# Graph tensor product on one core: table building beside the routing loops, and a chunk's spread emitted in two half-steps

## The chip, the cores and the metric

The kernel runs on one NeuronCore of one Trainium2 chip. The metric is the device time of one execution in microseconds (us), less is better. Below, PE is the tensor engine, DVE the vector engine, ACT the scalar engine, POOL the GpSimd engine and SP the engine that issues most plain DMAs. "L547" is line 547 of the kernel before.

## The reference

There are N = 10000 nodes with 64 channels of 4 components each, and E = 640000 edges with random source and destination. Each edge carries 4 components `Y` and 4 features.

```python
R = _silu(edge_feat @ w_rad)                              # (E, C)
xs = x[src]                                               # (E, C, M)
tp = jnp.einsum('eci,ef,ifo->eco', xs, Y, cg)             # (E, C, M)
msg = R[:, :, None] * tp
agg = _segment_sum(msg.reshape(-1, C * M), dst, N).reshape(N, C, M)
return jnp.einsum('ncm,cd->ndm', agg, w_mix)
```

The costly parts are the gather by `src` and the sum by `dst`, both over random indices.

## The kernel before

The edges are first sorted by destination, in two passes, so that the sum by destination becomes dense matrix products over buckets of 32 nodes. A record of an edge is 9 words: a key that packs source and destination, `Y`, and the features.

**Three splits.** The edges are cut into three splits (0.3, 0.355 and 0.345 of them). Each split goes through pass 1, pass 2 and the messages, and later splits add to the sums of earlier ones.

**Pass 1** (`pass1`) sorts the records of a split into 18 groups of 576 nodes in DRAM (`grp`), and **pass 2** (`pass2`) sorts each group into 18 buckets (`bkt`). Together a (split, group) pair is called a segment. There are 54 segments, and the small group of 7 buckets comes first in each split.

**Tables and route.** Both passes have the same two parts. `tables` (L306 to L462) computes from digit counts where each row of output goes. It is a serial chain of small steps: a matmul on PE into the one PSUM tile with the tag `misc`, a copy by ACT or DVE, some small DVE operations of 18 to 400 columns, the next matmul. The four matmul groups that matter here are `cnt` (L320), `prep` (L341 to L343), `stp` (L404) and `ovp` (L444 to L446). As `misc` has one buffer, a stream takes it with `bank` (L135) and gives it back by setting `held` to None; the final mix of the messages uses it too. `route` (L464) then goes over chunks of 12 (pass 1) or 11 (pass 2) tiles of 128 records. Per chunk, `spread` (L516) makes a slot mask (DVE, L521), the spread records X (DVE, L524), and one-hot rows `oh` (half of them on DVE, L533, the others on ACT as six squares, L539, and one Relu, L540); a step later `move` (L543) multiplies them on PE, then `evict` copies the result out of PSUM (ACT, L554), and `store` writes it by an indirect DMA on POOL (L558). `places` (L475) holds a second one-buffer PSUM tile, with the lock `pos`, from an odd step to the next even one. X and `oh` have three buffers each, shared by the two passes.

**Messages** (`messages`, L737) run over 939 units, one per bucket and split, of 5 or 6 tiles each. Per unit POOL gathers x by source (L781), DVE builds S (L815, L818) and the products with the radial factor (L825), PE sums into PSUM (L836), DVE or ACT takes the sums out (L865, L867), and in the last split PE mixes the channels (L884). A unit is emitted in four quarters.

**Order.** In the first phase (`p1`), which runs pass 1 of the first split, only SP has a hand-written order; the other engines are ordered by a planner. The clears of `bkt` and of the later groups are woven in on SP: 0.75 clears for each step that the pass yields. In the second phase (`p2`), PE, DVE and ACT execute strictly in the order in which the generators are stepped in `groups` (L916). Before each quarter of the messages, pass 1 of the next split is advanced as far as its due time asks (counted in chunks), and pass 2 of the next segment by its share of `pass2_steps`; a step's yield says its weight, 4 (`HEAVY`) for a chunk. In pass 2, a segment's tables are built first and its route runs after them. In pass 1, the tables of the next block are advanced between the chunks, without a yield of their own when they are not yet needed. The third phase (`p3`) handles overflowing records in two short loops.

## Time and profile before

| | |
|---|---|
| time, median of 3 runs | 10816.96 us (10789.08 to 10847.26) |
| profiled execution, its own time | 10910.27 us |
| its span, first to last instruction | 10908.5 us |
| PE busy | 8286.5 us, 76% of the span |
| DVE busy | 6989.5 us, 64% |
| POOL busy | 6043.2 us, 55% |
| ACT busy | 4039.2 us, 37% |
| granted PE clock, mean | 0.84 |
| DMA traffic | 1057.34 MB, mean 97 GB/s |

Busy times are of one profiled execution; a group's row gives busy time, mean duration of one instruction, then the idle time of its engine just before it and what ended most of that idle time. No engine is busy throughout, so what matters is which waits follow each other.

### The profile page before, as it was taken

How to read it: one execution, taken by the hardware profiler on the slowest of the kernel's cores; microseconds unless marked ns; L12 is line 12 of the kernel's file. 1: busy time of each engine (PE TensorE's matmuls, PEld its weight loads, DVE VectorE, ACT ScalarE, POOL GpSimd, SP SyncE). 2: the span in 40 equal slices, each digit the busy share in tenths (PEclk: the TensorE clock that was granted, in tenths of full speed). 3: DMA queues.
4: the chain of work that ended last, by engine and by line, in shares of the span. 5: the costliest groups of instructions: out<-in, count | busy, mean ns of one | idle time of the engine just before them, and what ended most of it. 6: DMA issues, size and time to landing. Idle time of an engine off the chain costs nothing. (4 is left out here: it accounts for less than half of the span.)

```text
span 10908.5 us, 147397 instructions
## 1 busy us (share of the span) xinstructions
PE 8286.5 (76%) x51381; PEld 6957.6 (64%) x51381; DVE 6989.5 (64%) x12762; ACT 4039.2 (37%) x11789; POOL 6043.2 (55%) x6306
## 2 busy tenths in 40 slices
PE   6867777777777777777777777777778787878775
PEld 5756666666666566666666666656666666666664
DVE  7866667766666576666676666656555555555553
ACT  6743444444443353333343334322223232322220
POOL 1235555555555555555555555665666666665664
PEclk9977888888888788888888888878888888888887
DMA  7212233333332323333333333333333333333332
GB/s 167 73 54 86 85 94 91 92 89 89 89 93 85 97 84 99 102 98 103 105 101 102 107 95 100 104 109 106 104 101 101 100 99 102 99 102 97 100 100 74
DMA packets 696319, 1057.34 MB, mean 97 GB/s; under 512 B 251979, under 2 KB 500327, under 8 KB 695576
## 3 DMA queue, kind: packets, MB, share of 16 engines
q0 software_dynamic: 286560, 746.72, 23.6%
q1 hardware_dynamic: 406424, 293.41, 9.6%
q8 instruction: 407, 6.67, 0.3%
q10 hardware_dynamic: 2592, 7.78, 0.2%
q14 instruction: 336, 2.75, 0.1%
HBM read 856.49 MB, written 207.52 MB: 98 GB/s over the span
## 5 line engine op out<-in xcount | busy, mean ns | idle before, releaser
L781 POOL DMA_INDIRECT xg<-in_x_dram,sidx x5321 | 5069.7, 953 | 3389.2 <-issue 1380.6
L547 PE MATMUL pr<-X,oh 128*128 128x135 f32 (+1 forms) x21286 | 3144.8, 303 | 798.8 <-issue 518.9
L547 PEld LDWEIGHTS pr<-X,oh 128*128 128x128 f32 x21286 | 2883.6, 211 | 1153.8 <-issue 800.7
L836 PE MATMUL G<-S,xg 128*128 128x128 f32 x21284 | 3116.0, 310 | 584.6 <-issue 197.1
L836 PEld LDWEIGHTS G<-S,xg 128*128 128x128 f32 x21284 | 2988.0, 225 | 683.4 <-issue 236.5
L524 DVE TENSOR_TENSOR X<-dv,Wt 128x1512 f32<-128x1512 f32 (+4 forms) x958 | 1600.7, 1671 | 619.1 <-remote 299.1
L825 DVE TENSOR_TENSOR xg<-xg,pre 128x1536 f32<-128x1536 f32 (+1 forms) x939 | 1556.5, 1658 | 418.6 <-ACT pre L807 266.9
L539 ACT ACTIVATE sq<-i,rowf 128x128 f32<-128x128 f32 x5658 | 1750.8, 392 | 74.0 <-DVE rowf L511 65.2
L807 ACT ACTIVATE pre<-pre 128x384 f32<-128x384 f32 (+1 forms) x939 | 428.9, 457 | 2110.8 <-remote 756.3
L804 PE MATMUL pre<-wr,sT 54*128 54x384 f32 (+1 forms) x1878 | 936.6, 582 | 165.8 <-ACT sT L799 127.1
L540 ACT ACTIVATE oh<-sq,ones 128x768 f32<-128x768 f32 (+2 forms) x958 | 937.4, 978 | 191.1 <-remote 61.1
L818 DVE TENSOR_TENSOR S<-dv,pay 128x768 f32<-128x768 f32 (+1 forms) x939 | 857.4, 913 | 139.9 <-remote 64.0
L558 POOL DMA_INDIRECT bkt<-rt,idx x541 | 542.7, 1003 | 600.4 <-ACT rt L554 402.3
L865 DVE TENSOR_TENSOR Gs<-old,G 128x256 f32<-128x256 f32 x313 | 131.8, 421 | 1143.8 <-remote 474.5
L558 POOL DMA_INDIRECT grp<-rt,idx x417 | 416.0, 998 | 782.7 <-ACT rt L554 391.0
L533 DVE TENSOR_TENSOR oh<-dv,rowf 128x640 f32<-128x640 f32 (+2 forms) x922 | 800.5, 868 | 0.4 <-remote 0.4
L554 ACT ACTIVATE rt<-pr 128x135 f32<-128x135 f32 (+1 forms) x958 | 258.6, 270 | 892.4 <-remote 378.0
L865 DVE TENSOR_TENSOR Gp<-old,G 128x256 f32<-128x256 f32 x313 | 131.0, 419 | 622.8 <-remote 361.0
L494 ACT ACTIVATE pc<-pp 128x396 f32<-128x396 f32 (+3 forms) x506 | 244.8, 484 | 731.4 <-PE pp L486 334.4
L804 PEld LDWEIGHTS pre<-wr,sT 54*128 54x128 f32 (+1 forms) x1878 | 311.0, 207 | 311.6 <-ACT sT L799 139.3
L884 PE MATMUL po<-wf,Gs 128*128 128x256 f32 (+2 forms) x1392 | 405.5, 456 | 54.4 <-ACT colsbkt L325 38.5
L884 PEld LDWEIGHTS po<-wf,Gs 128*128 128x128 f32 (+2 forms) x1392 | 298.2, 220 | 178.0 <-issue 78.2
(214 smaller groups left out, 5101.1 us busy)
## 6 DMA issues: line engine op xcount, KB each, us to landing
xg<-in_x_dram,sidx POOLq DMA_INDIRECT x5321
sums<-Gp SPq DMA_DIRECT2D x626, 128.0 KB
old<-sums SPq DMA_DIRECT2D x626, 128.0 KB
bkt<-z SPq DMA_DIRECT2D x24, 994.5 KB
pay<-bkt SPq DMA_DIRECT2D x34, 486.0 KB
ys<-in_Y_dram SPq DMA_DIRECT2D x104, 96.0 KB
es<-in_edge_feat_dram SPq DMA_DIRECT2D x104, 96.0 KB
out_dram<-ot SPq DMA_DIRECT2D x69, 128.0 KB
```

The costliest lines, as they stand in the source:

```text
L524: nc.vector.tensor_tensor(X[:, :m, :].rearrange("p t (s w) -> p t s w", w=W), msk.unsqueeze(3).to_broadcast([P, m, ps.r, W]), QD[c // Q][1 ...
L533: nc.vector.tensor_tensor(oh[:, :v, :], self.v128.unsqueeze(1).to_broadcast([P, v, P]), row[:, o:o + v].unsqueeze(2).to_broadcast([P, v, P ...
L539: nc.scalar.activation(sq[:, u, :], self.i128, AF.Square, bias=to, scale=-1.0)
L540: nc.scalar.activation(oh[:, v:v + len(at), :], sq[:, :len(at), :], AF.Relu, bias=self.ones[:, 0:1], scale=-2.0)
L547: nc.tensor.matmul(pr[:, :ps.rw], oh[:, u, :], X[:, u, :], start=(u == 0), stop=(not on and u == m - 1))
L558: st = nc.gpsimd.indirect_dma_start(out=ps.dst, out_offset=bass.IndirectOffsetOnAxis(ap=idx[:, i:i + 1], axis=0), in_=RT.pop(c), in_offset ...
L781: nc.gpsimd.indirect_dma_start(out=xg[:, t, :], out_offset=None, in_=self.x, in_offset=bass.IndirectOffsetOnAxis(ap=si[:, u:u + 1], axis=0))
L804: nc.tensor.matmul(R, ST_.pop(k)[:ut * W], self.wr[:ut * W, :ut * 64], start=True, stop=True)
L818: nc.vector.tensor_tensor(S[:, :ut], self.eq[:, :ut].unsqueeze(3).to_broadcast([P, ut, NB, 4]), pb[:, :, 1:5].unsqueeze(2).to_broadcast([P ...
L825: nc.vector.tensor_tensor(V, V, R.unsqueeze(3).to_broadcast([P, ut, 64, 4]), op=OP.mult)
L836: nc.tensor.matmul(G[:, h].rearrange("p n f -> p (n f)"), V[:, t, 32 * h:32 * h + 32, :].rearrange("p c i -> p (c i)"), S[:, t].rearrange( ...
L884: nc.tensor.matmul(po[:nn, :256], Gs[:, h, f].rearrange("p b n -> p (b n)")[:, :nn], self.wf[:, h, f, :], start=(h + f == 0), stop=(h + f ...
```

## The change

- `tables` yields once more before each of the matmul groups `prep`, `stp` and `ovp`, ahead of taking the `misc` tile.
- `spread` is cut in two: mask and X first, then a yield ("half"), then the one-hot rows in a new `rows`. The weight of the chunk's step is split into 2 and 2.
- In `pass1`, each step of a block's tables yields by itself, and a stream that holds `misc` goes on at once.
- In `pass2`, `front` (digits and tables of the next segment) is a side stream: it is stepped between the half-steps of the current segment's route. D2 gets a second buffer. The next segment's records are loaded at the start of the current route.
- `groups` paces pass 1 by weights, not by chunks; `pass2_steps` counts accordingly; the first segment of a new split is due 22 quarters earlier.
- The clears of the first phase are woven in at 0.5 for each yield instead of 0.75.
- In the overflow loop, the duplicate test and the gather of the current output row move ahead of the radial part.

```diff
@@ tables
             self.floor(R[:H], n[:H], r, True, ps.key, H)
+        yield
         yield from self.bank(ps.key)
         pre_p = ...
...
+        yield
         yield from self.bank(ps.key)
         st_p = ...
...
+        yield
         yield from self.bank(ps.key)
         ov_p = ...
@@ route
         def spread(c):
-            row, slot = MS[c // (2 * Q)]
+            _, slot = MS[c // (2 * Q)]
...
+            XO[c] = X
+
+        def rows(c):
+
+            row, _ = MS[c // (2 * Q)]
+            o = c % (2 * Q) * T
+            m = min(T, nt - c * T)
             (_, _, _, tg), i = table(c)
...
-            XO[c] = (X, oh, m, on)
+            XO[c] = (XO[c], oh, m, on)
...
             if 0 <= k < N:
                 spread(k)
+                yield "half"
+                rows(k)
...
-            yield HEAVY if 0 <= k < N + lag else 1
+            yield (HEAVY - 2 if k < N else HEAVY) if 0 <= k < N + lag else 1
@@ pass1
-            if side is not None and (need or acc >= 1.0):
+            if side is not None and (need or acc >= 1.0 or self.held == ps.key):
                 acc -= 1.0
                 said = next(side, "end")
                 if said == "end":
                     side = None
-                elif need:
-                    yield said
-                elif said == "held":
-                    acc = 0.0
-                continue
+                    continue
+                yield said
+                if need or said != "held":
+                    continue
+                acc = 0.0
             said = next(route, "end")
             if said == "end":
                 break
+            if said == "half":
+                yield 2
+                continue
@@ pass2
-        nxt = None
-        for i, (k, g) in enumerate(self.segs):
...
+        ready = {}
+
+        def front(i, Wt):
...
-            D = ph.tile([P, M, B], BF, name="D2", bufs=1)
+            D = ph.tile([P, M, B], BF, name="D2", bufs=2)
             yield
             yield from self.digits(D, dg, nt)
-            nxt = load(*self.segs[i + 1]) if i + 1 < len(self.segs) and self.segs[i + 1][0] == k else None
             yield from self.tables(ps, D, nt, kc, self.kov[:, 1:2], base, self.bc)
-            tab = self.tab[ps.key]
-            yield from self.route(ps, lambda t, m: (D[:, t:t + m], Wt[:, t:t + m]), nt, lambda c: (tab, c))
+            ready[i] = D, Wt, self.tab[ps.key]
+
+        for i, (k, g) in enumerate(self.segs):
+            nt, nb = self.gt[k][g], min(B, self.NBK - g * B)
+            if i not in ready:
+                yield from front(i, load(k, g))
+            D, Wt, tab = ready.pop(i)
+
+            side = None
+            if i + 1 < len(self.segs) and self.segs[i + 1][0] == k:
+                side = front(i + 1, load(*self.segs[i + 1]))
+            for said in self.route(ps, lambda t, m: (D[:, t:t + m], Wt[:, t:t + m]), nt, lambda c: (tab, c)):
+                if said == "held":
+                    if self.held == ps.key:
+                        side = self.go(side)[0]
+                    yield said
+                    continue
+                said = 2 if said == "half" else said
+                n = said - 1 if said > 1 else 1
+                yield 1
+                for _ in range(n):
+                    if side is not None:
+                        side, at = self.go(side)
+                        if at == "held":
+                            yield at
+                            break
+                    yield 1
+            while side is not None:
+                side, at = self.go(side)
+                yield at
...
+    @staticmethod
+    def go(side):
+
+        said = next(side, "end") if side is not None else "end"
+        return (None, None) if said == "end" else (side, said)
+
     def pass2_steps(self, k, g):
         nch = (self.gt[k][g] + self.p2.T - 1) // self.p2.T
-        return (self.gt[k][g] + 23) // 24 + 12 + self.p2.carry + 6 + self.ls + HEAVY * nch
+
+        return 2 * (8 + self.ls) + HEAVY * nch + 20 * ((k, g) == self.segs[k * self.NG])
@@ groups
+        for k in range(1, len(SPLIT)):
+            ends[k * NG - 1] -= 22
+
...
-            later.append((self.pass1(k, self.p1.NC), at, end, self.chunks(k) + 6 + self.ls))
+            n = self.chunks(k)
+            later.append((self.pass1(k, self.p1.NC), at, end, HEAVY * n + 20 * (n / (self.p1.NC - 2) + 2)))
             at = end
-        self.done = -6
+        done = 0.0
         while segs[0] not in self.pay:
             next(sort)
             if later:
-                next(later[0][0])
+                said = next(later[0][0])
+                done += 0.0 if said == "held" else said or 1
...
-                while self.done + 6 < n * (v + 1 - at) / (end - at) or due:
+                while done < n * (v + 1 - at) / (end - at) or due:
                     due = False
                     said = next(first, "end")
...
                     if said in ("held", "end"):
                         break
+                    done += said or 1
@@ overflow, body: opd, oeq, odup, oskip, oem, odi, ocur and its gather (L1040 to L1068)
@@ now stand between the gather of oxg and the transpose of pay; nothing else changes there
@@ run
-                run(weave(first, later, 0.75))
+                run(weave(first, later, 0.5))
```

More of the change, by code (lines that the diff above doesn't have):

```diff
@@ L701, in load @@
             return Wt
-        nxt = None
-        for i, (k, g) in enumerate(self.segs):
-            nt, Wt = self.gt[k][g], nxt
-            if Wt is None:
-                Wt = load(k, g)
-            nb = min(B, self.NBK - g * B)
+        ready = {}
+        def front(i, Wt):
+            k, g = self.segs[i]
+            nt = self.gt[k][g]
             base = ph.tile([P, B], F, name="base")
@@ L1018, in body @@
                 in_offset=bass.IndirectOffsetOnAxis(ap=si, axis=0))
+            pd = pm_.tile([P, 512], F, name="opd", tag="misc", bufs=1)
+            nc.tensor.matmul(pd[:, :P], dst.to_broadcast([P, P]), self.ident, start=True, stop=True)
+            eq = wk.tile([P, P], F, name="oeq")
+            nc.vector.tensor_scalar(eq, pd[:, :P], dst, None, op0=OP.is_equal)
+            dup = wk.tile([P, P], F, name="odup")
+            nc.vector.tensor_tensor(dup, eq, self.L, op=OP.mult)
+            skip = wk.tile([P, 1], F, name="oskip")
+            nc.vector.tensor_reduce(skip, dup, axis=AX.X, op=OP.max)
+            em = wk.tile([P, 1], F, name="oem")
+            nc.vector.tensor_scalar(em, dst, 0.5, None, op0=OP.is_lt)
+            nc.vector.tensor_tensor(skip, skip, em, op=OP.max)
+            di = wk.tile([P, 1], I32, name="odi")
+            nc.vector.scalar_tensor_tensor(skip, skip, FAR, dst, op0=OP.mult, op1=OP.add)
+            nc.vector.tensor_scalar(di, skip, -1.0, None, op0=OP.add)
+            cur = wk.tile([P, 256], F, name="ocur")
+            nc.vector.memset(cur, 0.0)
+            nc.gpsimd.indirect_dma_start(
+                out=cur, out_offset=None, in_=self.out, in_offset=bass.IndirectOffsetOnAxis(ap=di, axis=0),
+                bounds_check=self.N - 1, oob_is_err=False)
             pT = pm_.tile([P, 512], F, name="opT", tag="misc", bufs=1)
```

23 lines of the change are left out of this document (2 added, 21 removed).

## The prediction

> **What bounds the kernel now.** I read the page's head, then the busy times by stage (the borders are mine: first phase, start of the second, the three splits of the messages, the overflow loops).
>
> ```profile
> span 10908.5 us, 147397 instructions
> PE 8286.5 (76%) x51381; PEld 6957.6 (64%) x51381; DVE 6989.5 (64%) x12762; ACT 4039.2 (37%) x11789; POOL 6043.2 (55%) x6306
> ```
>
> The stages' rows give start and end, length, busy time (and instructions) of PE, PEld, DVE, ACT and POOL, the granted PE clock, the DMA share and GB/s.
>
> ```profile
> 0.00:590.00 590.00, 449.48 (x3381) 393.60 (x3381) 482.19 (x1058) 407.75 (x1223) 124.61 (x139) 0.92 0.46 112
> 590.00:760.00 170.00, 85.51 (x482) 67.31 (x483) 105.14 (x313) 69.07 (x198) 47.03 (x49) 0.66 0.18 50
> 760.00:4000.00 3240.00, 2495.87 (x16010) 2133.83 (x16010) 2203.96 (x4107) 1402.01 (x4167) 1806.81 (x1877) 0.84 0.31 89
> 4000.00:7650.00 3650.00, 2766.81 (x17172) 2332.02 (x17173) 2411.17 (x4258) 1334.09 (x3846) 2117.57 (x2207) 0.84 0.35 102
> 7650.00:10836.00 3186.00, 2468.51 (x14277) 2018.37 (x14276) 1764.73 (x2930) 823.07 (x2344) 1935.91 (x2024) 0.84 0.34 100
> ```
>
> The three splits take 10076 of 10908.5 us. There PE is busy 2495.87 + 2766.81 + 2468.51 = 7731 us, 77%, more than any other engine. Its clock is 0.84 on the mean, so part of that busy time is slow time. The 939 units have 3756 quarters: one lasts 10076 / 3756 = 2.68 us and holds 7731 / 3756 = 2.06 us of PE work.
>
> Next, the count of products (L825) in two stretches of the last split, which has no pass 1 beside it: with pass 2 running, and after its end.
>
> ```profile
> 7650.00:10500.00 2850.00, 478.04 (x274) 0.85 0.34 100
> 10500.00:10829.00 329.00, 67.20 (x40) 0.80 0.35 104
> ```
>
> A unit takes 2850 / 274 = 10.4 us with sorting beside it and 329 / 40 = 8.2 us without. So the sorting costs what it interposes. Where, the groups of the stage 760 to 10836 show (busy time, mean ns, idle time before with its releasers).
>
> ```profile
> L781 POOL DMA_INDIRECT xg<-in_x_dram,sidx x5286 | 5036.4, 953 | 3359.4 <-issue 1370.3 <-PE G L836 951.3 <-remote 580.2
> L836 PE MATMUL G<-S,xg 128*128 128x128 f32 x21279 | 3115.4, 310 | 584.6 <-issue 197.1 <-DVE Gs L865 178.0 <-DVE Gp L865 132.8
> L404 PE MATMUL stp<-bs,onesb 11*128 11x209 bf16 (+5 forms) x74 | 23.4, 317 | 264.7 <-DVE bs L392 102.4 <-DVE dd L388 73.9 <-DVE dl L385 53.2
> L444 PE MATMUL ovp<-fl,Ub 128*128 128x11 bf16 (+5 forms) x74 | 12.5, 169 | 163.9 <-DVE fl L439 102.8 <-DVE un L438 28.6 <-DVE fl L434 18.5
> L341 PE MATMUL prep<-R,U 12*64 12x18 f32 (+3 forms) x46 | 7.0, 224 | 43.4 <-DVE R L304 39.5 <-DVE ri L303 3.7
> ```
>
> POOL's gathers need 5036.4 + 1370.3 = 6407 us and wait 951 us for PE to free their buffers, so PE leads there. The matmuls of the tables do almost no work, 23.4, 12.5 and 7.0 us, yet PE stands 264.7 + 163.9 + 43.4 = 472 us in front of them, always for small DVE operations. One table of pass 2, seen from PE:
>
> ```profile
> 9432.79 0.91 PE L804 MATMUL pre<-wr,sT 54*128 54x384 f32 x2
> 9438.42 0.35 PE L404 MATMUL stp<-bs,onesb 11*128 11x209 bf16 x1 [4.72 <-DVE bs L392]
> ...
> 9448.51 0.17 PE L444 MATMUL ovp<-fl,Ub 128*128 128x11 bf16 x1 [3.89 <-DVE fl L439]
> ```
>
> ```profile
> 9435.20:9442.00 6.80, 3.58 (x17) 3.40 (x18) 5.10 (x22) 0.62 (x2) 3.79 (x4) 0.51 0.33 99
> 9442.10:9445.50 3.40, 1.99 (x13) 1.47 (x13) 1.96 (x3) 0.00 (x0) 1.64 (x2) 1.00 0.08 18
> 9445.50:9455.70 10.20, 7.19 (x29) 5.97 (x29) 6.98 (x22) 0.83 (x3) 4.04 (x5) 0.50 0.27 84
> ```
>
> A gap of 4.72 us and one of 3.89 us, and about each of them the granted clock is 0.5 for 6.8 and 10.2 us. A table's gap is paid twice, as idle time and as slow work after it.
>
> **The change part by part.**
>
> *The three new yields and the side streams.* PE now gets other work between the DVE operations and the matmul that needs them: about one quarter, 2.06 us. There are 74 chains with `stp` and `ovp`, and the row of `prep` has 46 records in pairs, 23 chains. The mean waits are 264.7 / 74 = 3.6, 163.9 / 74 = 2.2 and 43.4 / 23 = 1.9 us. If all waits were equal, 74 x 2.06 + 74 x 2.06 + 43 = 348 us would go. They are unequal (4.72 and 3.89 here, others nothing), so I take three quarters, 260 us. Bounds: 0, if PE then stands at the next matmul that needs DVE; 472, if all goes.
>
> *Clock.* At 0.5 for 6.8 us PE loses 3.4 us of work. If one wait in each of the 74 chains is long enough, that is 74 x 3.4 = 252 us. A wait of 3.6 us shortened by 2.06 still leaves some of them, so I take half, 126 us. Bounds: 0, as other gaps slow the clock too, and 252.
>
> [...]
>
> *Half-steps.* A chunk's instructions on DVE, ACT and the wait rows of PE for them, same stage:
>
> ```profile
> L524 DVE TENSOR_TENSOR X<-dv,Wt 128x1485 f32<-128x1485 f32 (+4 forms) x817 | 1358.4, 1663 | 581.3 <-remote 267.3 <-PE pr L547 148.2 <-PE G L836 33.0
> L521 DVE TENSOR_TENSOR dv<-dv,slot 128x165 f32<-128x165 f32 (+3 forms) x816 | 271.8, 333 | 7.4
> L533 DVE TENSOR_TENSOR oh<-dv,rowf 128x640 f32<-128x640 f32 (+2 forms) x781 | 670.1, 858 | 0.4 <-remote 0.4
> L539 ACT ACTIVATE sq<-i,rowf 128x128 f32<-128x128 f32 x4812 | 1486.7, 392 | 34.3 <-DVE rowf L511 26.0 <-DVE row L509 6.4 <-DVE oh L533 1.8
> L540 ACT ACTIVATE oh<-sq,ones 128x768 f32<-128x768 f32 (+2 forms) x817 | 805.0, 985 | 190.6 <-remote 61.1 <-PE pr L547 35.4 <-PE pr L549 21.3
> ```
>
> ```profile
> PE pr L547 <- DVE oh L533: 6.1, 5, 2.2
> ...
> PE pr L547 <- ACT oh L540: 2.1, 1, 2.1
> ```
>
> The five groups give busy time, mean ns and idle time before; the last two are PE's waits (us in total, times, longest). No instruction is added. DVE's block of 0.33 + 1.66 + 0.86 = 2.85 us, longer than a quarter, becomes 2.00 and 0.86 us, so L865, which queues behind it and frees the sums for PE, comes sooner. PE waits 178.0 + 132.8 = 311 us for L865; I take off the share by which the block shrinks, 30%, 93 us. Bounds: 93 us more, as the rows now stand before another quarter's L865, and 311 less. ACT's block of squares is not cut: nothing there. The store on POOL moves half a step later with the rows; it still follows its copy by two steps, and POOL's 951 us of waits for PE cover it. The lock `pos` is now held over a half-step and a step instead of one step, so the other stream meets it closed more often; its cost is in the last rival.
>
> *Sum in the splits.* 260 + 126 + 93 = 479 us of PE time. Not all of PE's time sets the end; I take PE's busy share, 77%: 369 us.
>
> *Loads.* The next segment's records are now read by DVE right at the start of a route. SP's queue before at such a place, and what DVE waited for at that reader (L716) in the whole run:
>
> ```profile
> 9199.47 0.33 SPq L700 DMA_DIRECT2D Wt<-grp  x1
> ...
> 9216.36 0.38 SPq L728 DMA_DIRECT2D pay<-bkt  x1
> ```
>
> ```profile
>   DMA Wt<-grp: 2.1, 1
> ```
>
> The load goes out when the last read of its buffer ends, 17 us ahead of the payload's load, and the new reader comes after that payload. I take 0. What hides it is the last chunks' way through PE, ACT and POOL. Without that cover DVE, and L865 and the products queued behind it, would wait for a landing, once 2.1 us: 51 x 2.1 = 107 us. The second D2 buffer is what lets `front` write while the route still reads; no wait for it is added.
>
> *Start and split ends.* The second segment's tables now precede the first payload: the chain shown above lasted from 9432.79 to 9448.51 with other work in it, and there are some 28 more steps, each with up to half a chunk of pass 1 (1.43 us of DVE) beside it, which is only brought forward. I take +10, bounds 0 and 28 x 1.43 = 40. At the end of a split there is a hole:
>
> ```profile
> 3998.00:4024.30 26.30, 1.43 (x1) 0.76 0.36 96
> ```
>
> One product in 26.3 us, twice in the run. The earlier due time may fill part: -20, bounds -52 and +52.
>
> *First phase.* Work on DVE fills 482 of 590 us. A chunk now yields twice, and each table step once, so at 0.5 the clears come at 1 to 2 for each chunk where they came at 0.75: earlier and denser on SP.
>
> ```profile
> 114.18 43.87 SPq L241 DMA_DIRECT2D bkt<-z  x9
> ```
>
> ```profile
> 187.84 0.27 DVE L631 TENSOR_SCALAR key<-da 128x216 int32<-128x216 int32 x1 [32.38 <-DMA da<-in_dst_dram]
> ```
>
> Nine clears hold SP for 43.87 us, and the load of `da` behind them stops DVE, and all behind it, for 32.38 us. Denser clears are over sooner, but the early loads stand behind more of them: +15, bounds -32 and +60.
>
> *Overflow loops.* DVE waits for the gather of `ocur` in each of three rounds:
>
> ```profile
> L1069 DVE TENSOR_TENSOR ocur<-ocur,opo 128x256 f32<-128x256 f32 x3 | 1.3, 422 | 8.8 <-DMA ocur<-out_dram,odi 8.8
> ```
>
> The gather now runs beside the radial part, but PE's last product before this sum ends shortly before it too. Bounds -8.8 and 0; I take -3.
>
> **Total.** -369 + 10 - 20 + 15 - 3 = -367. The profiled execution's own time is 10910.27, 1.8 us around its span; 10910 - 367 = 10543. The median of the runs, 10816.96, is 0.9914 of the profiled time, so the forecast is 10450 us.
>
> **Rivals.**
>
> *All of it goes.* PE is released from all 472, 252 and 311 us: 1035 x 0.77 = 797, 10910 - 795 = 10115, times 0.9914 is 10030. For it: POOL's 6407 us and its 817 stores leave room. Against: the last engine to answer is DVE, and it has no less to do. Halfway from the forecast: 10240.
>
> *The waits move on.* PE reaches the next product or L865 earlier and stands there, because DVE's order still holds the same work; the three PE terms are 0 and the time is 10818. For it: the 311 us at L865 exist already. Against: the sorting-free stretch at 8.2 us shows that DVE's products alone do not hold PE. [...]
>
> *Late rows, slower.* The rows are now emitted half a step before `move`, and while the lock `pos` is held a stream is forced on each quarter. Then `move` follows its rows by 2.68 us, while they need 0.86 + 6 x 0.39 + 0.39 for the carried row + 0.99 = 4.6 us: PE stands 1.9 us. For half of the 817 chunks (the row of L524) that is 776 us, 598 on the path: 10910 - 367 + 598 = 11141, or 11050. It decides from 367 / (1.9 x 0.77) = 251 chunks on. Against: the lock forces steps already, and PE waits for rows only 6.1 + 2.1 us in the whole stage.
>
> **How the numbers follow.** A measurement here tells about 0.5% from no change. Forecast (its own range 10300 to 10700) 0.50; all goes 0.20; moves on 0.15; late rows 0.15. Faster: 0.50 + 0.20 and 0.02 of the third, 0.72; same 0.13; slower 0.15. The range reaches past the second rival's midpoint and a little beyond no change: 10150 to 10890.
>
> **What would show it.** The idle time before L404 and L444 falls from 429 us to about 200; the clock in the splits rises from 0.84 to 0.87 or so; idle before L836 for L865 falls below 250; PE's waits for `oh` stay under 50 us; units with sorting beside them take some 10 us. The forecast is wrong if those table waits fall and L836 or L547 gains as much, if waits for `oh` pass 300 us, or if the first phase ends after 650 us.

## The result and the profile after

| | before | after |
|---|---|---|
| time, median | 10823.97 us (10789.08 to 10847.26, 4 runs) | 10525.95 us (10515.35 to 10545.99, 4 runs) |
| ratio | | 0.9729, 95% interval 0.9699 to 0.976 |
| profiled execution, its own time | 10910.27 us | 10515.35 us |

The kernel is 2.7% faster. Every ratio in this document compares runs on one chip. The experiments ran on four chips; on two of these even the kernel before took under 8800 us, and on one of the two the change was measured again and gave 0.5%. What sets the pace in either case is shown below; why the chips differ stays open. The profiled execution of before is itself 0.9% above the median of its runs, so some 86 us of what lies between the two profiles belong to that execution and not to the change.

The head of the profile after:

```profile
span 10513.1 us, 147153 instructions
PE 8168.5 (78%) x51381; PEld 6902.7 (66%) x51381; DVE 6994.0 (67%) x12762; ACT 3989.1 (38%) x11789; POOL 6026.1 (57%) x6306
```

The same stages as in the prediction, with borders at the same events (length, then busy time and instructions of PE, PEld, DVE, ACT and POOL, the granted PE clock, DMA share and GB/s):

```profile
0.00:630.00 630.00, 463.79 (x3381) 407.82 (x3381) 481.31 (x1058) 407.41 (x1223) 125.00 (x139) 0.88 0.48 105
630.00:842.00 212.00, 117.62 (x723) 98.48 (x723) 147.75 (x423) 93.84 (x276) 50.76 (x53) 0.70 0.16 44
842.00:3930.00 3088.00, 2446.05 (x15866) 2103.33 (x15867) 2184.26 (x4069) 1372.79 (x4115) 1798.49 (x1873) 0.86 0.33 93
3930.00:7390.00 3460.00, 2707.62 (x17135) 2288.90 (x17134) 2412.95 (x4253) 1308.19 (x3829) 2109.74 (x2204) 0.85 0.38 108
7390.00:10443.00 3053.00, 2413.43 (x14219) 1991.93 (x14218) 1745.08 (x2865) 803.66 (x2335) 1931.15 (x2027) 0.85 0.37 105
```

The three splits now take 3088 + 3460 + 3053 = 9601 us where they took 10076: 475 us less. The two stages ahead of them are longer: 630 and 212 us where they were 590 and 170. DVE's busy time in the splits is the same to 1% (6342.3 us, where it was 6379.9). The clock in the splits is 0.86, 0.85 and 0.85, where it was 0.84 throughout.

PE's busy time in the splits is 2446.05 + 2707.62 + 2413.43 = 7567 us, 164 us less. Not all of that is the clock: the splits hold 239 matmuls fewer than before (47220 beside 47459), and the longer start holds 241 more (723 beside 482), which keep PE busy there for 117.62 - 85.51 = 32 us more. That leaves about 130 us, which I put down to the higher clock: an estimate from these rows, as no run changes the clock alone. The rest of the 475 us, 311 us, is idle time. Where it went, the groups of that stage show (busy, mean ns, idle time before with its releasers):

```profile
L885 PE MATMUL G<-S,xg 128*128 128x128 f32 x21281 | 3149.2, 309 | 781.6 <-issue 376.5 <-DVE Gs L914 241.3 <-DVE Gp L914 82.0
L557 PE MATMUL pr<-X,oh 128*128 128x135 f32 (+1 forms) x17800 | 2661.2, 306 | 729.1 <-issue 401.7 <-ACT rt L564 243.9 <-ACT oh L550 36.4
L406 PE MATMUL stp<-bs,onesb 11*128 11x209 bf16 (+4 forms) x73 | 19.0, 260 | 22.6 <-DVE bs L393 12.7 <-ACT tot L349 3.7 <-DVE dd L389 3.4
L447 PE MATMUL ovp<-fl,Ub 128*128 128x11 bf16 (+3 forms) x73 | 12.9, 177 | 14.6 <-DVE fl L441 7.6 <-DVE rk L456 1.7 <-DVE dest L431 1.4
L342 PE MATMUL prep<-R,U 12*64 12x18 f32 (+3 forms) x44 | 6.7, 227 | 6.7 <-DVE sums L330 3.2 <-issue 2.8 <-DVE R L304 0.7
```

The lines are renumbered: L885 is the sums (L836 before), L557 a chunk's products (L547), L406 `stp`, L447 `ovp`, L342 `prep`. PE stood 264.7 + 163.9 + 43.4 = 472 us in front of the last three and now stands 22.6 + 14.6 + 6.7 = 44 us. Summed over all matmuls of the tables (`cnt`, `gop` and `ddp` too), idle time falls from 632 to 131 us, 501 us less. Of this, 190 us came back in front of other matmuls: 197 in front of the sums, 56 in front of the chunks' products, less what fell elsewhere. In the last split alone PE stood 127.8 us in front of `stp` and `ovp` before, and now not at all.

### The profile page after: what moved, and what is told of

Its sections match the earlier page's. It is cut to its first block, busy times and chain, and to the rows that moved or that the text cites. A ratio compares the mean times of both kernels' runs of the same rounds, so it can differ in the third digit from the quotient of the medians.

```text
span 10513.1 us, 147153 instructions
## 1 busy us (share of the span) xinstructions
PE 8168.5 (78%) x51381; PEld 6902.7 (66%) x51381; DVE 6994.0 (67%) x12762; ACT 3989.1 (38%) x11789; POOL 6026.1 (57%) x6306
## 2 busy tenths in 40 slices
DMA packets 696316, 1057.32 MB, mean 101 GB/s; under 512 B 251979, under 2 KB 500327, under 8 KB 695576
## 5 line engine op out<-in xcount | busy, mean ns | idle before, releaser
L557 PE MATMUL pr<-X,oh 128*128 128x126 f32 (+1 forms) x21286 | 3139.1, 305 | 861.8 <-issue 417.4
L885 PE MATMUL G<-S,xg 128*128 128x128 f32 x21284 | 3149.5, 309 | 781.6 <-issue 376.5
L557 PEld LDWEIGHTS pr<-X,oh 128*128 128x128 f32 x21286 | 2915.3, 214 | 1110.4 <-issue 644.6
L885 PEld LDWEIGHTS G<-S,xg 128*128 128x128 f32 x21284 | 2983.8, 223 | 906.2 <-issue 459.2
L527 DVE TENSOR_TENSOR X<-dv,Wt 128x1485 f32<-128x1485 f32 (+4 forms) x958 | 1600.5, 1671 | 594.7 <-remote 246.6
L874 DVE TENSOR_TENSOR xg<-xg,pre 128x1536 f32<-128x1536 f32 (+1 forms) x939 | 1556.8, 1658 | 562.1 <-ACT pre L856 439.7
L853 PE MATMUL pre<-wr,sT 54*128 54x384 f32 (+1 forms) x1878 | 885.3, 552 | 188.5 <-ACT sT L848 125.2
L550 ACT ACTIVATE oh<-sq,ones 128x896 f32<-128x896 f32 (+2 forms) x958 | 937.5, 979 | 44.9 <-issue 13.8
L848 ACT ACTIVATE sT<-pre 54x128 f32<-54x128 f32 (+1 forms) x939 | 245.3, 261 | 596.2 <-PE pre L843 253.4
L843 PEld LDWEIGHTS pre<-ident,pay 128*54 128x54 f32 (+1 forms) x939 | 108.7, 116 | 424.5 <-issue 211.4
L933 PE MATMUL po<-wf,Gs 128*128 128x256 f32 (+2 forms) x1392 | 340.1, 393 | 28.0 <-issue 24.8
```

The source lines that it names most:

```text
L527: nc.vector.tensor_tensor(X[:, :m, :].rearrange("p t (s w) -> p t s w", w=W), msk.unsqueeze(3).to_broadcast([P, m, ps.r, W]), QD[c // Q][1 ...
L550: nc.scalar.activation(oh[:, v:v + len(at), :], sq[:, :len(at), :], AF.Relu, bias=self.ones[:, 0:1], scale=-2.0)
L557: nc.tensor.matmul(pr[:, :ps.rw], oh[:, u, :], X[:, u, :], start=(u == 0), stop=(not on and u == m - 1))
L853: nc.tensor.matmul(R, ST_.pop(k)[:ut * W], self.wr[:ut * W, :ut * 64], start=True, stop=True)
L874: nc.vector.tensor_tensor(V, V, R.unsqueeze(3).to_broadcast([P, ut, 64, 4]), op=OP.mult)
L885: nc.tensor.matmul(G[:, h].rearrange("p n f -> p (n f)"), V[:, t, 32 * h:32 * h + 32, :].rearrange("p c i -> p (c i)"), S[:, t].rearrange( ...
```

## The experiments

The first four ran on one chip, where the kernel before took 10910.01 us.

**1. The yields alone.** Edit, on the kernel before, ahead of `prep`, `stp` and `ovp`, and in the count of steps:

```diff
+        yield
         yield from self.bank(ps.key)
...
-        return (self.gt[k][g] + 23) // 24 + 12 + ...
+        return (self.gt[k][g] + 23) // 24 + 15 + ...
```

> The kernel before with the three yields alone (and three more steps in the count by which pass 2 is paced). Nothing of the computation is left out. Theory (yields are the whole gain): the idle time before stp, ovp and prep falls from 500 us to under 100, and the time to 10450 to 10560, at least as fast as the changed kernel because the first phase and the start keep their old length (84 us shorter to the first product). Rival (a yield without the streams only moves the wait to the next matmul that needs DVE): over 10720.

Measured: 11287.32 us, 1.0343 of the kernel before (1.0326 to 1.0359). It is slower. Groups of its main stage:

```profile
L550 PE MATMUL pr<-X,oh 128*128 128x135 f32 (+1 forms) x17896 | 2751.9, 308 | 1149.8 <-issue 589.5 <-ACT rt L557 510.8 <-DVE oh L536 26.8
L406 PE MATMUL stp<-bs,onesb 11*128 11x209 bf16 (+5 forms) x74 | 20.6, 279 | 118.0 <-DVE bs L393 44.6 <-DVE go L399 26.4 <-DVE dl L385 23.8
L447 PE MATMUL ovp<-fl,Ub 128*128 128x11 bf16 (+5 forms) x74 | 12.9, 175 | 27.2 <-DVE fl L436 17.1 <-DVE fl L441 4.4 <-DVE di L435 2.1
```

The yields do at the tables most of what they were meant to do: 118.0 us at `stp` and 27.2 at `ovp`, where it was 264.7 and 163.9. A part does move to the next matmuls of the tables, as the rival said: `gop` waits 103.2 us where it waited 30.9, and `ddp` 106.7 where it waited 78.5. Yet over all tables the wait still falls, from 632 to 427 us. What costs is the route: the chunks' products (L550) now wait 1149.8 us, where L547 of the kernel before waited 672.9. Of `gop`, the first row below is this run's; the other two are of the kernel before. Experiment 6 shows where the route's wait comes from.

```profile
L415 PE MATMUL gop<-bq,onesb 11*128 11x209 bf16 (+2 forms) x51 | 15.0, 294 | 103.2 <-ACT sts L409 89.6 <-issue 3.6 <-DVE bq L401 3.6
L413 PE MATMUL gop<-bq,onesb 11*128 11x209 bf16 (+2 forms) x51 | 14.2, 278 | 30.9 <-ACT sts L407 21.7 <-DVE bq L400 4.0 <-DVE go L399 1.8
L547 PE MATMUL pr<-X,oh 128*128 128x135 f32 (+1 forms) x17992 | 2705.9, 305 | 672.9 <-issue 499.4 <-ACT rt L554 144.0 <-DVE oh L533 6.1
```

**2. The change without the yields** at the same three places:

```diff
-        yield
         yield from self.bank(ps.key)
```

> The changed kernel without the three new yields in the tables; side streams, half-steps and pacing kept. Nothing of the computation is left out. Theory (the yields put a quarter of the messages between the small DVE operations and the matmul that needs them): PE's idle time before the matmuls of stp, ovp and prep goes back from 49 us to 400 us or more, the time from 10526 to 10750 or above. Rival (the streams themselves put other work there, or the half-steps gave the gain): that idle time stays under 200 us and the time under 10620.

Measured: 10699.02 us, 0.9811 (0.9798 to 0.9825). Two groups of its main stage:

```profile
L404 PE MATMUL stp<-bs,onesb 11*128 11x209 bf16 (+4 forms) x72 | 19.5, 271 | 104.9 <-DVE bs L392 71.3 <-DVE dd L388 11.3 <-issue 7.9
L444 PE MATMUL ovp<-fl,Ub 128*128 128x11 bf16 (+4 forms) x73 | 12.4, 170 | 123.2 <-DVE fl L439 53.4 <-DVE fl L434 28.8 <-DVE dest L429 10.5
```

104.9 and 123.2 us, and 22.2 at `prep`: 250 us, between the 472 of the kernel before and the 44 of the change. What is left of the change without the yields brings about half of the fall, and the yields bring the other half. That the half comes from the side streams, which spread a table's steps between other work, is the likely reading; the new pacing is in this run too and was not taken out by itself. Both expectations miss; time and waits lie between them.

**3. The change with pass 2's tables ahead of the route again.** `pass2` is that of the kernel before, which only turns the route's "half" into a weight, with the count of steps of experiment 1:

```diff
+            for said in self.route(ps, ...):
+                yield 2 if said == "half" else said
```

> The changed kernel with pass 2's tables again ahead of each route, one after the other, with the load ahead as before and one D2 buffer; the yields, the half-steps and pass 1's stream and pacing kept. Nothing of the computation is left out. Theory (yields, not streams): the main stage, from the first product on, is within 50 us of the changed kernel's 9594, the first product comes some 30 us earlier, since the second segment's tables no longer stand ahead of the first payload: 10470 to 10540 in all. Rival (the streams spread the tables' DVE work and so give the gain): 10620 or more, with PE's idle time at the tables back over 250 us.

Measured: 11141.85 us, 1.0204 (1.019 to 1.0218). The chunks' products of its main stage:

```profile
L557 PE MATMUL pr<-X,oh 128*128 128x135 f32 (+1 forms) x17896 | 2760.1, 308 | 1072.1 <-issue 606.3 <-ACT rt L564 362.9 <-ACT oh L550 47.6
```

Again it is not the tables that cost (162.6 us in front of `stp`, `ovp` and `prep`), but 1072.1 us in front of the chunks. My theory that the yields suffice fails in this form. It doesn't show that the streams are needed: here, too, the chunks fall in pairs on places where they fell in experiment 1, as experiment 5 tells, and experiment 6 gives the price of that.

**4. The change with the spread in one step.**

```diff
             if 0 <= k < N:
                 spread(k)
-                yield "half"
                 rows(k)
...
-            yield (HEAVY - 2 if k < N else HEAVY) if 0 <= k < N + lag else 1
+            yield HEAVY if 0 <= k < N + lag else 1
...
-                for _ in range(n):
-                    if side is not None:
+                for j in range(n):
+                    if side is not None and j != 1:
...
-                run(weave(first, later, 0.5))
+                run(weave(first, later, 0.75))
```

The middle edits keep the weight of a chunk and its two steps of the side stream; the last keeps about as many clears for each chunk as the kernel before had.

> The changed kernel with a chunk's spread in one step again (mask, X and one-hot rows together, one step of weight 4), side streams, yields and pacing kept; the clears of the first phase at 0.75 a step, about as many for each chunk as before. Nothing of the computation is left out. Theory (the gain comes from PE no longer standing at the tables' matmuls; the half-steps add nothing): the time stays within 40 us of the changed kernel's 10526, and PE's idle time before the products for L885 (the sums G of the changed kernel) stays within 40 us of its 324 us. Rival (the half-steps carry a part, as my prediction had it with 93 us or more of PE time): 10600 to 10700, with 400 us or more of idle time for that line.

Measured: 10572.57 us, 0.9688 (0.9675 to 0.9701). That is 46 us more than the change's 10526, just outside of the 40 us that the theory gave it, but on a chip where the kernel before took 86 us more too: by the ratio it is no slower than the change's 0.9729, whose interval it touches. The sums and `stp` of its main stage:

```profile
L884 PE MATMUL G<-S,xg 128*128 128x128 f32 x21284 | 3197.0, 313 | 788.1 <-issue 352.2 <-DVE Gs L913 221.0 <-DVE Gp L913 133.4
L406 PE MATMUL stp<-bs,onesb 11*128 11x209 bf16 (+5 forms) x72 | 19.4, 269 | 55.9 <-DVE bs L393 33.5 <-remote 9.3 <-DVE dd L389 8.8
```

PE waits 221.0 + 133.4 = 354 us for the eviction of the sums, where the change has 241.3 + 82.0 = 323 and the kernel before 311. So the half-steps may take 30 us off that wait, as the theory allowed, but no time comes of it.

**5. The change on another chip, and the place of the chunks.** On the next chip the kernel before took 8760.6 us.

> The changed kernel itself, as the measure for the other variants. All theories: 0.970 to 0.976 of the kernel before, as measured already.

Measured: 8710.64 us, 0.9949 (0.9935 to 0.9963). The expectation is wrong: there the change is worth 0.5%. Three groups of the whole run:

```profile
L885 PE MATMUL G<-S,xg 128*128 128x128 f32 x21284 | 2872.1, 297 | 89.3 <-DVE Gp L914 72.9 <-ACT Gp L916 8.8 <-DVE Gs L914 3.6
L557 PE MATMUL pr<-X,oh 128*128 128x126 f32 (+1 forms) x21286 | 2789.5, 289 | 369.0 <-ACT rt L564 211.2 <-DVE oh L543 120.5 <-DVE n L333 7.3
L874 DVE TENSOR_TENSOR xg<-xg,pre 128x1536 f32<-128x1536 f32 (+1 forms) x939 | 1558.0, 1659 | 882.5 <-DMA xg<-in_x_dram,sidx 670.7 <-ACT pre L856 140.5 <-ACT pc L497 28.8
```

and the last of them in the first profile of the change:

```profile
L874 DVE TENSOR_TENSOR xg<-xg,pre 128x1536 f32<-128x1536 f32 (+1 forms) x939 | 1556.8, 1658 | 562.1 <-ACT pre L856 439.7 <-DMA xg<-in_x_dram,sidx 57.6 <-issue 42.9
```

In front of the sums and the chunks no "issue" wait is among PE's three longest any more: these are 85.3 of 89.3 us and 339.0 of 369.0. Now DVE waits for gathers: 670.7 us at the products with the radial factor, where it was 57.6. POOL in the last split with pass 2 running, on this chip (5945 to 8269 us) and on the first (7256 to 10045 us):

```profile
L830 POOL DMA_INDIRECT xg<-in_x_dram,sidx x1675 | 1588.6, 948 | 512.7 <-issue 454.3 <-DMA bkt<-rt,idx 18.0 <-DMA xg<-in_x_dram,sidx 7.6
L568 POOL DMA_INDIRECT bkt<-rt,idx x171 | 171.7, 1004 | 52.1 <-issue 43.9 <-ACT pre L856 3.7 <-ACT sT L848 2.7
```

```profile
L830 POOL DMA_INDIRECT xg<-in_x_dram,sidx x1692 | 1604.8, 948 | 824.6 <-issue 448.6 <-remote 201.9 <-PE pre L843 75.5
L568 POOL DMA_INDIRECT bkt<-rt,idx x172 | 172.6, 1003 | 187.7 <-ACT rt L564 101.6 <-issue 45.6 <-DVE dv L524 21.1
```

Here POOL's gathers and stores with their issue time need 1588.6 + 454.3 + 171.7 + 43.9 = 2258 of 2324 us, 97%; on the first chip 1604.8 + 448.6 + 172.6 + 45.6 = 2272 of 2789 us, 81%. On this chip POOL sets the pace of this stretch: in the 2309 us from 5960 to 8269 PE is busy 2010.76 us, 87%, and DVE 1636.97, 71%. What a wait that PE saves at the tables is worth then, the segments below show: 3 us less of such waits in each, and 0.5 us between them.

The other three kernels of this chip tested the place of the chunks in a unit. A reading of the instruction order had shown this: the lock `pos` forces the step after an odd one into the next quarter, so chunks 1 and 2, 3 and 4, 5 and 6 of a route come in pairs, one quarter apart. In the kernel before the pairs fall on quarters 0 and 1, and the unit's sums lie between. In experiment 1 the yields shift them by one quarter, to 1 and 2: in PE's order of the last split three pairs in each of 15 segments, 45, stand with no sum between their two chunks, in experiment 3 there are 45 too, in the kernel before and in the change none.

The first of the three is experiment 1 with the old places:

```diff
-        return (self.gt[k][g] + 23) // 24 + 15 + ...
+        return (self.gt[k][g] + 23) // 24 + 12 + ...
...
-                    i, start, acc = i + 1, ends[i], 0.0
+                    i, start, acc = i + 1, ends[i], 3.0
```

> The kernel before with the three yields, and with pass 2 paced so that its route falls on the same quarters as in the kernel before: a segment's first three steps (digits) are taken at once, and the count of steps stays the old one. Without this the yields put the pairs of chunks of a route on the quarters 1 and 2 of one unit, where the kernel before has them on 0 and 1, with the sums G between them. Nothing of the computation is left out. Theory (place of the chunks: the yields gain at the tables, and what they lost was the place of the chunks): a segment of the last split takes 176 to 182 us, where the yields alone took about 199 and the kernel before 188; the time 0.96 to 0.98 of the kernel before. Rival (the yields themselves cost, since the route has one unit less for its chunks): no faster than the kernel before, 1.00 to 1.035 of it.

The second is the change with four places in turn, the third the same with the spread in one step as in experiment 4:

```diff
-                acc += self.pass2_steps(*segs[i + 1]) / (ends[i] - start)
+                acc += 1.0
...
-                    i, start, acc = i + 1, ends[i], 0.0
+                    i, start, acc = i + 1, ends[i], -0.5 - (i + 1) % 4
```

> The changed kernel with pass 2 at exactly one step for each quarter, and each segment's start put off by 0 to 3 quarters in turn, so that in the last split the first half-steps of a route fall all on quarter 1, 2, 3 or 0 of a unit, for four segments each. Nothing of the computation is left out. Theory (the place decides): the four kinds of segment differ by 6 us or more of some 176 us, quarter 0 or 3 best, just ahead of the sums G and the longest stretch of PE's work. Rival (only the pairs cost, the place of a chunk that stands alone does not): all four within 3 us of each other.

> The same with a chunk's spread in one whole step (mask, X and rows together), the clears at 0.75 a step. Nothing of the computation is left out. Theory (a half-step only gives more freedom in place): the best of the four whole-step kinds is within 2 us of the best half-step kind, and the worst is worse than the worst half-step kind, since all 2.85 us of DVE fall together. Rival (half-steps help by themselves): each whole-step kind is slower than the half-step kind with the same start by 3 us or more.

Measured: 1.0033 (1.0021 to 1.0044) for the first; 8682.51 and 8636.95 us (one run each, 0.991 and 0.986 of the kernel before) for the others. The segments of the last split (from a product's start to that 18 units later) take 150 us in the first, 149 to 151 in the second and 150 in the third, whatever the place, and 149.7 in the change. With POOL as the bound the question can't be answered there. It shows how little PE's waits count there: in their main stages the first kernel has these waits, the change those below it:

```profile
L406 PE MATMUL stp<-bs,onesb 11*128 11x209 bf16 (+5 forms) x74 | 20.9, 283 | 183.2 <-DVE bs L393 183.2
L447 PE MATMUL ovp<-fl,Ub 128*128 128x11 bf16 (+5 forms) x74 | 12.5, 169 | 133.3 <-DVE fl L441 93.6 <-DVE fl L436 39.8
```

```profile
L406 PE MATMUL stp<-bs,onesb 11*128 11x209 bf16 (+4 forms) x73 | 19.1, 261 | 65.8 <-DVE bs L393 44.7 <-ACT tot L349 19.1 <-DVE sts L426 2.0
L447 PE MATMUL ovp<-fl,Ub 128*128 128x11 bf16 (+3 forms) x73 | 12.7, 174 | 17.0 <-DVE fl L436 8.6 <-DVE fl L441 8.0 <-ACT colsbkt L325 0.3
```

These are 316.5 us against 82.8 in the main stage. Of them 51.7 us and none lie in the last split, 3 us for each of its segments, and the segments differ by 0.5 us. The first two splits, where POOL's share was not measured, are 37 and 25 us shorter in the change.

The first two ran on another chip too, which proved to be of the same kind (8775.89 us for the kernel before).

> The kernel before with the three yields and the old quarters for the chunks, once more: the earlier run of it fell on a chip on which every variant's segments of the last split take 149 to 151 us, so that it could not tell. Theory (place of the chunks), on a chip where the kernel before takes 10800 us or more: 0.96 to 0.985 of the kernel before, a segment of the last split 176 to 184 us. Rival (the yields themselves cost): 1.00 to 1.035, and 190 to 200 us. On a chip like the last one: 1.00 again.

> The changed kernel with each segment's chunks on one quarter, in turn 1, 2, 3 and 0, once more for the same reason. Theory (the place decides), on a chip where the kernel before takes 10800 us or more: the four kinds of segment differ by 6 us or more, quarter 0 or 3 best. Rival (only pairs in one unit cost): all four within 3 us of each other, near 178 us. On a chip like the last one: 149 to 151 us for all.

Measured: 1.0029 (1.0018 to 1.0041) and 0.992 (0.9902 to 0.9938), all segments 149 to 152 us again: what was expected for such a chip, and no answer.

**6. The four places in one kernel.** The last chip took 10814.25 us for the kernel before. The edit is to experiment 1, with the old count of steps (12) and, from segment to segment, another start:

```diff
-                    i, start, acc = i + 1, ends[i], 0.0
+                    i, start, acc = i + 1, ends[i], 3.0 - (i + 1) % 4
```

> The kernel before with the three yields, and each segment's first steps taken so that the pairs of chunks of its route fall on the quarters 0 and 1, 1 and 2, 2 and 3, or 3 and 0 of a unit, in turn, four segments each in the last split. Nothing of the computation is left out. On a chip where the kernel before takes 10800 us or more: theory (the place decides) the kind on 0 and 1 takes 176 to 184 us, the kind on 1 and 2 12 us or more longer; rival (the yields cost wherever the chunks fall) all four within 4 us, at 192 to 202 us. On a chip where it takes 8800 us or less, POOL's queue hides the place: all four at 149 to 152 us.

Measured: 1.0212 (1.0193 to 1.023). Five segments of its last split in order of time, with the pairs on quarters 0 and 1, 1 and 2, 2 and 3, 3 and 0, 0 and 1:

```profile
9733.64:9911.24 177.60, 145.62 (x884) 117.69 (x882) 106.65 (x182) 52.14 (x149) 113.92 (x121) 0.88 0.39 109
9911.24:10104.41 193.17, 150.18 (x845) 123.16 (x845) 106.16 (x182) 50.78 (x145) 112.30 (x119) 0.82 0.32 94
10104.41:10298.73 194.32, 151.62 (x854) 122.55 (x853) 106.35 (x182) 51.07 (x148) 112.41 (x119) 0.82 0.34 96
10298.73:10491.17 192.44, 149.81 (x828) 122.24 (x828) 108.55 (x186) 50.80 (x147) 114.88 (x121) 0.80 0.33 95
10491.17:10662.36 171.19, 139.85 (x846) 114.58 (x846) 104.28 (x176) 51.47 (x147) 108.94 (x115) 0.87 0.36 103
```

Beside them two segments of the kernel before, on its chip:

```profile
10156.21:10343.75 187.54, 147.53 (x854) 119.98 (x853) 107.06 (x183) 51.65 (x147) 113.74 (x119) 0.85 0.33 97
10343.75:10532.85 189.10, 145.83 (x849) 118.47 (x848) 105.84 (x178) 51.78 (x147) 114.00 (x119) 0.85 0.33 96
```

With the same yields, a segment takes 177.6 and 171.2 us where the pairs have the sums between them, and 192.4 to 194.3 us where they haven't. Over the last split the four places take on the mean 174.4 (four segments), 199.7, 189.5 and 190.7 us (three each). In experiment 1, with all pairs on 1 and 2, a segment takes 198 us on the mean, so little is carried from one segment to the next. The place decides, and the rival is refuted: on 0 and 1 the yields gain some 12 us of the 187 that a segment of the kernel before takes on the mean. The change, with streams and no pairs, takes 178 us: for these segments the yields alone, at the right place, give as much.

In front of the chunks' products (L550, and L552 for a carried tile) PE waits 5.8 and 3.9 us in the two fast segments above, and 12.6, 22.4 and 19.4 us in the three slow ones. The edit shifts all steps of a segment, those of the tables too, so what is shown is the place of the segment; that the pairs are what it acts by rests on these waits and on PE's order. The clock tells part of it, 0.87 and 0.88 against 0.80 to 0.82: PE is busy 150.5 us on the mean of the three and 142.7 on that of the two, with about as many instructions, and idle for some 11 us more.

**7. A version that may beat both.**

```diff
-                yield "half"
                 rows(k)
...
-                said = next(later[0][0])
+            turn = not turn
+            if later and turn:
+                said = next(later[0][0])
...
-                acc += self.pass2_steps(*segs[i + 1]) / (ends[i] - start)
+                acc += 1.0
...
-                run(weave(first, later, 0.5))
+                run(weave(first, later, 0.35))
```

Beside these, the weight of a chunk and its steps of the side stream are as in experiment 4.

> A version that may beat both: the changed kernel with a chunk's spread in one whole step, pass 2 at exactly one step for each quarter, pass 1 of the next split advanced only at every second step of the start, and the clears of the first phase at 0.35 a step. Nothing of the computation is left out. On a chip where the kernel before takes 10800 us or more: theory (streams and even pace are the gain; the half-steps give nothing, and the start and the clears give back some 40 us) 0.955 to 0.967 of the kernel before; rival (these edits do nothing) 0.969 to 0.976. On a chip where it takes 8800 us or less, where POOL's queue sets the pace of the last split: theory 0.978 to 0.988, rival 0.992 to 0.997.

Measured, on the chip of experiment 6: 10404.09 us, 0.9632 (0.9617 to 0.9646), within the theory's range (0.955 to 0.967) and clear of the change's interval (0.9699 to 0.976), which is of another chip. First phase, start and main stage:

```profile
0.00:588.50 588.50, 457.91 (x3381) 402.67 (x3381) 481.91 (x1057) 406.96 (x1223) 123.67 (x138) 0.91 0.49 112
588.50:764.00 175.50, 95.23 (x523) 77.84 (x524) 116.74 (x361) 76.25 (x220) 49.95 (x52) 0.68 0.18 49
764.00:10331.50 9567.50, 7607.90 (x47419) 6424.50 (x47419) 6359.28 (x11248) 3493.79 (x10333) 5842.80 (x6104) 0.85 0.36 103
```

588.5 + 175.5 us to the first product, where the change takes 630 + 212: 78 us of the gain. The main stage is 9567.5 us beside 9601. The four edits were not separated.

## Why the prediction came out

It said 10450 us, faster, and the time is 10526, 2.7% less: right in sign, within its own range of 10300 to 10700. That the sum came within 28 us of the profiled execution (10543 and 10515) is in part luck: the splits fell by 86 us more than it had with the split ends (475 for 369 + 20), start and first phase grew by 57 us more, and the execution of before was a long one. By its steps:

- **Table waits, -260 of 472.** The mechanism was right, the size too small: 428 of the 472 went. I took a mean quarter of 2.06 us against unequal waits. A yield is not the only thing that separates the steps, though. Experiment 2 shows that the rest of the change, without the yields, removes about half of these waits, which my reasoning left out.
- **Clock, -126.** Of the 164 us by which PE's busy time fell in the splits, about 130 are the clock's by the estimate above, close to the half of 252 that I took. How long a wait must be for the clock to fall, no run here shows, so that half was an estimate too. The trace has the granted clock at 0.5 for 2784 us of the splits, where it was 3217, though the waits at the tables fell from 472 to 44 us; so most of the time at 0.5 doesn't come from these waits, and what it comes from was not shown.
- **Half-steps, -93 of 311.** This step failed. The wait for the eviction is 323 us, not below 250, and experiment 4 finds no time in the half-steps.
- **The factor 0.77.** It stood for work that doesn't set the end. Of 501 us freed at the tables 190 came back as other idle time, so 0.62 of it counted, and the busy time counted in full: 311 + 164 = 475, where I had 369. Some 32 of the 164 us only moved into the start.
- **Start and first phase, +10 and +15.** They are 42 and 40 us longer, and of the 42 the work that moved out of the splits is a part, as the forecast had it. Experiment 7, which halves pass 1's steps at the start and thins the clears, gets both back. For the first phase the cause is less sure. The waits for `da`, which I had blamed, are the same in sum (before, then three rows of the change):

```profile
L631 DVE TENSOR_SCALAR key<-da 128x144 int32<-128x144 int32 (+6 forms) x31 | 8.1, 260 | 61.4 <-DMA da<-in_dst_dram 61.4
```

```profile
L643 DVE TENSOR_SCALAR key<-da 128x144 int32<-128x144 int32 (+6 forms) x31 | 7.7, 247 | 59.5 <-DMA da<-in_dst_dram 59.5
L731 DVE TENSOR_SCALAR dg<-Wt 128x97 int32<-128x97 int32 (+5 forms) x54 | 14.2, 264 | 4.6 <-DMA Wt<-grp 4.6
L1124 DVE TENSOR_TENSOR ocur<-ocur,opo 128x256 f32<-128x256 f32 x3 | 1.3, 422 | 11.8 <-PE opo L1122 11.8
```

and the same kernel's first phase ended at 606.5 us on one chip and at 624.1 on another of the same kind. Some 18 of the 40 us may therefore be no effect of the change. (It is the first kernel of experiment 5, on its two chips.) The half-steps and streams aren't needed for the rest: with the three yields alone and the old 0.75 clears, in experiments 1 and 6, the phase ended at 618.3 and 618.8 us, and on the chip of the latter at 588.5 with 0.35 clears. So the likely cause is that more yields bring the clears earlier, as the forecast said; the edits of experiment 7 were not separated.
- **Loads, 0.** Right: `dg` (L731) waited 4.6 us for its records in the whole run.
- **Split ends, -20.** This step failed too. I read the hole at the first border as standing twice in the run; from one product to the next it was 26.4 us at the first border and 13.6 at the second. Now it is 21.0 (row below) and 18.2, so the two together gave 1 us:

```profile
3932.00:3953.00 21.00, 1.50 (x2) 0.67 0.39 100
```

- **Overflow, -3.** DVE's wait for the gather of `ocur` is gone, as the row of L1124 above shows; it waits 11.8 us for PE instead. The tail behind the last sum went from 72.5 to 70.1 us.
- **Late rows.** That rival didn't come: the waits for `oh` in the whole run are

```profile
PE pr L557 <- DVE oh L543: 91.5, 36, 54.1
PE pr L557 <- ACT oh L550: 39.1, 19, 5.1
```

of which 54.1 us are one wait in the first phase. The other 76 us are more than the 50 I allowed, and far from the 300 that would have marked the rival.
- **From the profile to the median.** In its own terms the forecast was 10543 us, and the profiled execution took 10515. What missed was the last step, times 0.9914: the profiled execution of before lay 0.9% above the median of its runs, that of after 0.1% below. The 395 us between the two profiles are 298 us between the medians.

"The waits move on" was the right rival for another kind of chip. On the chips of experiment 5, where POOL is at 97% in the stretch measured, the time stayed at 0.986 (one run) to 1.003 whatever PE waited for. On the first chip, with PE at 77% in the splits before and POOL at 81%, no work was taken out, and the time fell by 2.7%.

Not tried: the kernel before with yields and the old places throughout, on a chip where it takes 10800 us. By the 174.4 us of experiment 6 it might come near experiment 7 without any stream; that stays open, and so does what the new pacing is worth by itself.

## What to carry to other kernels

A yield put into one generator shifts every later step of its stream against the others. Where two streams meet with a period, as chunks and units here, look at the new places, not at the removed wait alone: with the same three yields a segment took 174 or 200 us, by one quarter of a unit, where it took 187 without them. And look for the second engine in line before you count a gain: where POOL was at 97% of the stretch measured, the same change gave 0.5% and not 2.7%.

## What was unexpected of the hardware

The same program took 10526 us on one chip and 8711 us on another. Instructions of DVE, ACT and POOL last equally long on both (the products of L874 1658 and 1659 ns, a square on ACT 391 ns, a gather 950 ns). What differs in the two profiles is PE, in two ways. Its clock is 0.851 on the first and 0.913 on the second. And on the first it stands, in bursts, with nothing to wait for that the profile shows, as in this row of sums (start, length, instructions, idle time before):

```profile
4455.28 0.36 PE L885 MATMUL G<-S,xg 128*128 128x128 f32 x1 [0.46 <-issue]
4455.98 0.27 PE L885 MATMUL G<-S,xg 128*128 128x128 f32 x1 [0.33 <-issue]
4457.38 0.39 PE L885 MATMUL G<-S,xg 128*128 128x128 f32 x2 [1.13 <-issue]
4458.11 0.27 PE L885 MATMUL G<-S,xg 128*128 128x128 f32 x1 [0.33 <-issue]
4459.52 1.29 PE L885 MATMUL G<-S,xg 128*128 128x128 f32 x3 [1.15 <-issue]
```

By the program the products of a unit read what one DVE operation each has written for all of them, S and xg, and the first of the unit had already run. Yet these rows start 0.7, 1.4, 0.7 and 1.4 us apart. In front of the sums such idle time is 376.5 us, and in front of the chunks 401.7 us, in the rows of the main stage above; on the second chip neither group of the change has any among its three longest waits. What causes it, the runs here don't tell: the program is the same, and both profiles have 696316 DMA packets and 1057.32 MB. As far as these runs tell, it goes with what a change of this kind is worth: with it PE is the busiest engine of the splits, at 77% before, and the change gave 2.7%; on the second chip POOL is at 97% of the stretch measured, and it gave 0.5%.
